# Transposing the last stage's first token group with TensorE, inside an expert's second product, in place of a DMA transpose

## The chip, the cores and the metric

The kernel runs on one core of a Trainium2 chip. The metric is the device time of one execution in microseconds (us). A core has five engines with a queue of instructions each: TensorE (PE; its weight loads are listed as PEld), VectorE (DVE), ScalarE (ACT), GpSimd (POOL) and SyncE (SP). Each works through its own queue in order and waits for others by semaphores; DMA transfers are issued from SP, ACT and POOL.

## The reference

Three stages, on 4 x 576 = 2304 tokens of 512 features:

```python
# 1. sparse attention: scores within tau of the row's maximum stay, then softmax, then @ v
# 2. sticky mixture of experts (8 experts, 512 -> 1024 -> 512): a token takes its own argmax
#    expert or keeps the one of the token before it
out[b, s] = p[e] * (np.maximum(x[b, s] @ w1[e], 0.0) @ w2[e])
# 3. feed-forward with a normalization ahead of it and a residual
mu = np.mean(x, axis=-1, keepdims=True)
var = np.mean((x - mu) ** 2, axis=-1, keepdims=True)
xn = (x - mu) / np.sqrt(var + 1e-06) * g_ln
ch = np.maximum(xn @ w_ch1, 0.0) @ w_ch2          # 512 -> 2048 -> 512
return x + ch
```

## The kernel before, in words

All products are made from pairs of float16 numbers: a value is split into a high part (ACT, a copy with a scale) and the rest (DVE, value minus high part), and a product takes three matmuls (high by high, high by rest, rest by high).

The order of work on each engine is the order in which the Python code records it; the tile pools add the waits on buffers. The part around the change is the loop over `i` in `range(ND0)`, six *single* units `u = E + i` (units 8 to 13). A unit is 128 tokens, sorted by expert, of one expert:

- `s1_unit(u, k)`, for `k` 0 and 1: four blocks of 128 hidden columns each of the first product (line 1012, PE, into a PSUM bank `a`, of which the pool `pa` has four). ACT writes the high part of `hid` (line 1016), DVE the rest (line 1017).
- `t_unit(u + 1)`: the next unit's gathered rows `xg` are transposed by TensorE from float32 (line 987, four transposes into one bank `a`), and split into `xT` by ACT (line 988) and DVE (line 989).
- `s2_unit(u, 0, ...)`: the second product, 24 matmuls into a bank `y` (line 1033), three for each of eight blocks of hidden columns. The first of the three takes the high part of `hid`, the second the rest. Then ACT scales `y` into `yb` (line 1039), and POOL scatters `yb` into the DRAM buffer `ys_d` (line 1041).
- `drip(n)`: brings up to `n` parts of later units' weights in. A part is a float32 block `stg` that a DMA of SP has loaded (lines 199 and 203; the pool has five such buffers), which ACT and DVE split into `w` (lines 124 and 125); the freed buffer is loaded again at once. Now and then the part is half of a block of the last stage's weights `fw`: three DVE steps on `xn` (lines 142, 144, 146), and at the next call of `drip` its split by ACT (line 179) and DVE (line 180), which the list `late` holds.

The last stage takes the tokens in `NG` = 9 groups of 256. For a group `g`, `f_load` reads it from `ys_d` into `xf`, `f_norm` makes mean and reciprocal deviation (DVE and ACT, lines 1080 to 1092), `f_split` normalizes each 128 tokens into `xn` (DVE, line 1101) and splits them into the float16 pair `f16` (ACT line 1102, DVE line 1103), and `f_x` transposes that pair by one DMA issued from ACT's queue into `nT` (line 1109). `halve(2 * g)` makes the first product from `nT` (`f_1`, line 1123: eight banks `a`, 24 matmuls each, with ACT line 1126 and DVE line 1127 behind each), and records the load, normalization and transpose of group `g + 1` on the way. `halve(2 * g + 1)` makes the second product (`f_2`, line 1136), adds the residual (line 1140) and scatters to the output (line 1141).

Units and halves alternate: unit 8, unit 9, half 0, unit 10, half 1, unit 11, half 2, and so on. The first group has no half ahead of it in which to be prepared: its load stands ahead of unit 8, and its normalization, split and transpose inside unit 9 (`i == 1`). From there half 0 begins as soon as unit 9's second product is issued and `nT` is written.

Of the kernel before, what the change touches and what calls it, by code (L numbers as in the profile page):

```python
# [8 lines left out]
F32 = mybir.dt.float32  # L9
F16 = mybir.dt.float16  # L10
I32 = mybir.dt.int32
BF16 = mybir.dt.bfloat16
AF = mybir.ActivationFunctionType
ALU = mybir.AluOpType
# [6 lines left out]
def kernel(  # L21
# [15 lines left out]
    nc = tc.nc  # L37
    B, H, S, D = q.shape
    E, DM, F = w1.shape
# [24 lines left out]
    ident = const.tile([128, 128], F32, name="ident")  # L64
# [119 lines left out]
    P, wt = {}, {}  # L184

    def weights(u, n):

        if (u, n) not in wt:
            sh = [128, 2, DM // 128, F] if n == 0 else [128, 2, F // 128, DM]
            nm = f"w{n}{u % 2}"  # L190
            wt[u, n] = P["wb_p" if u % 2 else "wa_p"][n].tile(sh, F16, name=nm, tag=nm)
        return wt[u, n]
# [37 lines left out]
    if True:  # L230
# [536 lines left out]
        for w, slot in enumerate((0, 1, 2, 3, 4, 5, 7, 8, 9, 11, 12)):  # L767
            for a in range(2):
                g = []
# [23 lines left out]
    V = nc.vector  # L793
# [96 lines left out]
    def tiles(u):  # L890

        if u in PAIRS:
            return PAIRS[u]
        return (2 * u, 2 * u + 1) if u < E else (E + u,)
# [4 lines left out]
    def gather(u):  # L899
        us[u, "g"] = []  # L900
        for n, c in enumerate(tiles(u)):
            xg = P["xgs"][u % 2 if single(u) else n]
            ix, R = (etb, NT - S) if u == "a" else (P["tb"], NT)
            nc.gpsimd.indirect_dma_start(
                out=xg[:], out_offset=None, in_=x_d[0:R, :], in_offset=bass.IndirectOffsetOnAxis(ap=ix[:, c:c + 1], axis=0),
                bounds_check=R - 1, oob_is_err=False)
            us[u, "g"].append(xg)
# [12 lines left out]
    for u in range(E + ND0):  # L920
        fq += [(u, j) for j in range(8)]
        n = 0 if u == 0 else 1
# [6 lines left out]
    def more(n=1):  # L929
        for _ in range(min(n, len(fq))):  # L930
            k = fq.pop(0)
            if k[0] == "f":
                parts[k] = ffn_half(*k[1:])
            else:
                fetch(*k)

    late = []

    def drip(n=1):

        if late:
            next(late.pop(), None)
        for _ in range(n):
            for k in pq:
                if k[0] == 1 and "wb_p" not in P:
                    return
                if k in parts and (not late if k[0] == "f" else k[0] < 2 or (k[0] - 2, k[1] // 4) in done):
                    break
                if k[0] != "f":
                    return  # L950
            else:
                return
            pq.remove(k)
            if k[0] == "f":
                late.append(parts.pop(k))
                next(late[0])
            else:
                parts.pop(k)()
            more()
# [13 lines left out]
    def ready(u, n):  # L973
        while (u, 4 * n + 3) in pq:
            drip()
# [4 lines left out]
    def t_unit(u):  # L980

        new_x(u)
        x = us[u, "x"]
        for n, xg in enumerate(us.pop((u, "g"))):
            t = P["pa"].tile([128, 4, 128], F32, name="a")
            for c in range(4):
                nc.tensor.transpose(t[:, c, :], xg[:, 128 * c:128 * c + 128], ident)
            nc.scalar.activation(out=x[:, 0, n], in_=t, func=AF.Copy, scale=64.0)
            V.scalar_tensor_tensor(out=x[:, 1, n], in0=t, scalar=64.0, in1=x[:, 0, n], op0=ALU.mult, op1=ALU.subtract)
# [29 lines left out]
    def s2_steps(u, i, between=lambda: None):  # L1019
        hid = us[u, "h"]  # L1020
        two = u in PAIRS
        wu = i if two else u
        t2 = weights(wu, 1)
        c = tiles(u)[i]
        if i == 0 or two:
            ready(wu, 1)
        if (two or i + 1 == len(tiles(u))) and u != "a":
            done.add((wu, 1))
        ps = P["py"].tile([128, DM], F32, name="y")
        n = 0  # L1030
        for f in range(8):
            for x, a in ((0, 0), (1, 0), (0, 1)):
                nc.tensor.matmul(ps, hid[:, x, f, 128 * i:128 * i + 128], t2[:, a, f, :], start=(n == 0), stop=(n == 23))  # L1033
                n += 1
            yield
        between()
        tb, tp, dx = (etb, etp, edx) if u == "a" else (P["tb"], P["tp"], P["didx"])
        yb = P["u_p"].tile([128, DM + 1], F32, name="yb", bufs=2)
        nc.scalar.activation(out=yb[:, 0:DM], in_=ps, func=AF.Copy, scale=tp[:, c:c + 1])
        nc.gpsimd.tensor_copy(out=yb.bitcast(I32)[:, DM:DM + 1], in_=tb[:, c:c + 1])  # L1040
        nc.gpsimd.indirect_dma_start(
            out=ys_d[:], out_offset=bass.IndirectOffsetOnAxis(ap=dx[:, c:c + 1], axis=0),
            in_=yb[:], in_offset=None, bounds_check=NT - 1, oob_is_err=False)

    def s1_unit(u, k):
        for _ in s1_steps(u, k):
            pass

    def s2_unit(u, i, between):
        for _ in s2_steps(u, i, between):  # L1050
            pass
# [16 lines left out]
    fs = {}  # L1068
# [6 lines left out]
    def f_norm(g):  # L1075
# [16 lines left out]
        V.reciprocal(out=rs, in_=rs)  # L1092
        fs[g, "n"] = (mv, rs)

    def f_split(g):
        xf = fs[g]
        mv, rs = fs.pop((g, "n"))
        n16 = P["n_p"].tile([128, 2, 2, DM], F16, name="f16")
        for t in range(2):
            xn = P["n_p"].tile([128, DM], F32, name="xn", tag="xn")  # L1100
            V.tensor_scalar(out=xn, in0=xf[:, t, 0:DM], scalar1=mv[:, t, 0:1], scalar2=rs[:, t:t + 1], op0=ALU.subtract, op1=ALU.mult)
            nc.scalar.activation(out=n16[:, 0, t], in_=xn, func=AF.Copy, scale=4.0)
            V.scalar_tensor_tensor(out=n16[:, 1, t], in0=xn, scalar=4.0, in1=n16[:, 0, t], op0=ALU.mult, op1=ALU.subtract)
        fs[g, "s"] = n16

    def f_x(g):
        n16 = fs.pop((g, "s"))
        nT = P["f_p"].tile([128, 2, 2, 4, 128], F16, name="nT")
        nc.scalar.dma_start_transpose(out=nT.rearrange("p a t c n -> p (a t c) n"), in_=n16.rearrange("p a t d -> p (a t d)"))
        fs[g, "x"] = nT  # L1110
# [36 lines left out]
    def halve(h, known=0):  # L1147

        g, b = divmod(h, 2)
        if b == 0:  # L1150
            for fb in range(8):
                f_1(g, fb)
                if fb < 5: drip()
                if g < NG - 1:
                    if fb == 1 and g >= known: f_load(g + 1)
                    if fb == 5 and g >= known: f_norm(g + 1)
                    if fb == 6: f_split(g + 1)
            if g < NG - 1:
                f_x(g + 1)
        else:  # L1160
            f_2(g, 0, drip)
            f_2(g, 1, drip)

    with tc.manual_schedule():
# [35 lines left out]
        g = -1  # L1200
# [72 lines left out]
        while bgp:  # L1273
            n = len(bgp)
# [34 lines left out]
        for i in range(ND0):  # L1309
            u = E + i  # L1310
            for k in range(2):
                s1_unit(u, k)
                if i == 1:
                    if late:
                        next(late.pop(), None)
                    (f_norm, f_split)[k](0)
                drip(1)
            if i + 1 < ND0:
                t_unit(u + 1)
                if i == 1:  # L1320
                    f_x(0)
                if i + 3 < ND0:
                    gather(u + 3)
            s2_unit(u, 0, lambda: drip(2))
            if i:
                halve(i - 1)
        for h in range(ND0 - 1, 2 * NG):
# [3 lines left out]
        def rest(i):  # L1331

            u = E + i
            with tc.If(nd > i):
                with tc.manual_schedule():
                    gather(u)
                    for j in range(5):
                        fetch(u, j)
                    t_unit(u)
                    for j in range(8):  # L1340
                        parts.pop((u, j))()
                        if j < 3:
                            fetch(u, j + 5)
                    for k in range(2):
                        s1_unit(u, k)
                    s2_unit(u, 0, lambda: None)
                    if i + 1 < NDYN:
                        rest(i + 1)
                    if i == ND0:
                        f_load(0)  # L1350
                        f_load(1)
                        f_norm(1)
                        f_norm(0)
                        f_split(0)
                        f_x(0)
                        for h in range(2 * NG):
                            halve(h, 1)
# [31 lines left out]
```

## Time and profile before

| | us |
|---|---|
| median of 3 runs | 1061.17 |
| lowest, highest | 1057.99, 1061.48 |
| the profiled execution | 1058.6 |
| its span, first to last instruction | 1056.8 |
| TensorE busy | 991.1 |
| VectorE busy | 653.4 |
| ScalarE busy | 505.6 |
| TensorE's wait for `nT` of group 0 | 6.2 |

The 1.8 us by which the profiled execution is longer than its span lie around the program's instructions. TensorE is busy for 94% of the span; where it stands still, all others have room, so what counts is what it waits for. Times in the rows are from the start of the span.

### The profile page before, as it was taken

To read this page: it belongs to the slowest core of one execution; us is meant where nothing else is said; L and a number is where in the kernel's file an instruction comes from. 1 tells how busy PE (TensorE), PEld (TensorE's weight loads), DVE (VectorE), ACT (ScalarE), POOL (GpSimd) and SP (SyncE) were. 2 spreads that over 40 slices of the span, in tenths; PEclk is the share of its full clock that TensorE was granted. 3 is DMA by queue.
4 is the path that set the end of the run, shared out by engine and by line. 5 is a ranking of instruction groups with operands and counts; after the bars stand their busy time and mean duration, and the time that the engine had idled before them with its cause. 6 is when DMAs were issued, how large, how long until landed. Compare 5 with 4: busy or idle time off the path is not lost. (4 is left out here: it accounts for less than half of the span.)

```text
span 1056.8 us, 23743 instructions
## 1 busy us (share of the span) xinstructions
PE 991.1 (94%) x9938; PEld 729.0 (69%) x9938; DVE 653.4 (62%) x1127; ACT 505.6 (48%) x791; POOL 391.1 (37%) x411
## 2 busy tenths in 40 slices
PE   6899998998999888899999979999999999999995
PEld 3678877787888776766677657584758668577572
DVE  7788888988897778797787667273334133131220
ACT  4688786786777665465576545243212011111010
POOL 3699897797788671352222300101000000000000
PEclk8999999999999999999999989999999999999998
DMA  7556544464442747578889755364111210111100
GB/s 178 140 136 158 131 103 126 116 156 133 106 93 47 193 134 225 189 241 283 267 298 292 263 181 158 120 205 117 37 31 31 61 31 31 44 37 41 30 12 23
DMA packets 124533, 137.34 MB, mean 130 GB/s; under 512 B 67450, under 2 KB 88954, under 8 KB 124416
## 3 DMA queue, kind: packets, MB, share of 16 engines
q1 hardware_dynamic: 98336, 116.43, 38.2%
q0 software_dynamic: 4960, 14.17, 3.7%
q10 hardware_dynamic: 21120, 5.13, 2.3%
q8 instruction: 79, 1.29, 0.5%
q14 instruction: 38, 0.31, 0.1%
HBM read 100.17 MB, written 19.94 MB: 114 GB/s over the span
## 5 line engine op out<-in xcount | busy, mean ns | idle before, releaser
L1123 PE MATMUL a<-nT,fw 128*128 128x256 f16 x1728 | 191.5, 274 | 6.2 <-DMA nT<-f 6.2
L459 POOL TENSOR_TENSOR hl<-em,hl 128x576 f16<-128x576 f32 x128 | 169.5, 1325 | 54.0 <-ACT hl L458 52.8
L1123 PEld LDWEIGHTS <-fw 128*128 128x128 f16 x1728 | 169.7, 98 | 28.6 <-issue 6.7
L1136 PE MATMUL y<-fw,hid 128*128 128x512 f16 x864 | 187.9, 379 | 0.0
L1136 PEld LDWEIGHTS <-hid 128*128 128x128 f16 x864 | 84.6, 98 | 100.4
L125 DVE SCALAR_TENSOR_TENSOR w<-stg,w 128x1024 f16<-128x1024 f32 x112 | 135.3, 1231 | 17.3 <-ACT w L124 16.6
L1126 ACT ACTIVATE hid<-a 128x512 f16<-128x512 f32 x72 | 42.7, 593 | 214.9 <-PE a L1123 213.0
L446 ACT ACTIVATE e<-s,t 128x576 f32<-128x576 f32 x144 | 106.1, 737 | 70.3 <-PE s L441 57.6
L1141 POOL DMA_INDIRECT out_dram<-xf x18 | 19.1, 1059 | 311.7 <-DVE xf L1140 311.7
L1012 PE MATMUL a<-xT,w 128*128 128x128 f16 (+1 forms) x1536 | 121.5, 241 | 1.5 <-DVE w L125 0.9
L1033 PE MATMUL y<-w,hid 128*128 128x512 f16 x528 | 117.7, 379 | 3.8 <-DVE hid L1017 3.3
L1012 PEld LDWEIGHTS <-w 128*128 128x128 f16 x1536 | 112.3, 99 | 11.3 <-DVE w L125 1.0
L403 DVE TENSOR_REDUCE mc<-sm 128x1 f32<-128x576 f32 x138 | 103.6, 751 | 24.8 <-PE sm L399 22.8
L124 ACT ACTIVATE w<-stg 128x1024 f16<-128x1024 f32 x112 | 114.5, 1051 | 7.7 <-DMA stg<-in_moe_w_dram 3.8
L452 DVE SCALAR_TENSOR_TENSOR em<-s,e 128x576 f32<-128x576 f32 x144 | 107.1, 745 | 9.7 <-POOL hl L459 8.5
L1127 DVE SCALAR_TENSOR_TENSOR hid<-a,hid 128x512 f16<-128x512 f32 x72 | 49.6, 688 | 101.5 <-ACT hid L1126 101.5
L1140 DVE SCALAR_TENSOR_TENSOR xf<-y,xf 128x512 f32<-128x512 f32 x18 | 12.5, 692 | 146.7 <-PE y L1136 146.7
L399 PE MATMUL sm<-qkt 128*128 128x288 f16 (+1 forms) x308 | 75.4, 291 | 24.3 <-DVE mc L403 21.4
L458 ACT ACTIVATE hl<-em 128x576 f16<-128x576 f32 x128 | 86.9, 679 | 18.9 <-DVE em L452 18.5
L1033 PEld LDWEIGHTS <-hid 128*128 128x128 f16 x528 | 50.9, 98 | 63.3 <-DVE hid L1017 5.1
L436 PE MATMUL s<-qkt 128*128 128x288 f16 (+1 forms) x320 | 90.2, 290 | 3.8 <-DVE em L452 3.1
L441 PE MATMUL s<-th,ind 128*128 128x128 bf16 (+5 forms) x960 | 92.0, 206 | 0.0
(290 smaller groups left out, 1797.6 us busy)
## 6 DMA issues: line engine op xcount, KB each, us to landing
stg<-in_moe_w_dram SPq DMA_DIRECT2D x112, 512.0 KB
stg<-in_moe_w_ch_dram SPq DMA_DIRECT2D x32, 512.0 KB
ys_d<-stg SPq DMA_DIRECT2D x6, 769.5 KB
xf<-ys_d SPq DMA_DIRECT2D x9, 513.0 KB
x_d<-xc SPq DMA_DIRECT2D x16, 256.0 KB
ku<-qkt SPq DMA_DIRECT2D x28, 144.0 KB
rawq<-in_q_dram SPq DMA_DIRECT2D x7, 512.0 KB
rawk<-in_k_dram SPq DMA_DIRECT2D x7, 512.0 KB
```

Of the source, the lines that this page charges most:

```text
L124: nc.scalar.activation(out=dst[:, 0, n], in_=t, func=AF.Copy, scale=scale)
L125: nc.vector.scalar_tensor_tensor(out=dst[:, 1, n], in0=t, scalar=scale, in1=dst[:, 0, n], op0=ALU.mult, op1=ALU.subtract)
L403: nc.vector.tensor_reduce(out=mcs[p % 2][:, j:j + 1], in_=mms.pop((p, j))[:, W0:W0 + 576], op=ALU.max, axis=AX.X)
L436: mm(o[:, W0 + 288 * c:W0 + 288 * c + 288], (kt, ku)[k][:, n], y, start=(k == 0), stop=False)
L441: mm(o[:, W0 + i:W0 + i + w], ind[:, t % 4, 0:o.shape[0]], y, start=False, stop=(i == of[-1][0]))
L446: nc.scalar.activation(out=e, in_=mst[p, j][:, W0:W0 + 576], func=AF.Exp, bias=t0, scale=SC)
L452: nc.vector.scalar_tensor_tensor(out=em, in0=ps[:, W0:W0 + 576], scalar=0.0, in1=e, op0=ALU.is_ge, op1=ALU.mult)
L459: nc.gpsimd.tensor_tensor(out=hl[:, 1], in0=em, in1=hl[:, 0], op=ALU.subtract)
L1012: nc.tensor.matmul(ps[:, f, :], t1[:, a, c, fc], x[:, h, i:i + N // 128, c, :], start=(n == 0), stop=(n == 11))
L1033: nc.tensor.matmul(ps, hid[:, x, f, 128 * i:128 * i + 128], t2[:, a, f, :], start=(n == 0), stop=(n == 23))
L1123: nc.tensor.matmul(ps[:, f, :], fw1[:, a, c, fc], x[:, h, :, c, :], start=(n == 0), stop=(n == 11))
L1136: nc.tensor.matmul(ps, hid[:, x, f, ts_], fw2[:, a, f, :], start=(n == 0), stop=(n == 47))
```

## The change

In unit 9 (`i == 1`), `f_split(0)` gives way to `f_rows(0)`: the two normalizations on DVE write float32 rows into one tile, and nothing is split there. `f_x(0)` goes. In its place `f_turn(0)` is recorded inside unit 9's second product, behind the fifth of its eight blocks: eight transposes by TensorE from the float32 rows, four into each of two banks `a`, and for each bank a split into `nT` by ACT and DVE, with the factor 4 that `f_split` applied. The call that finished a `late` half ahead of `f_norm` and `f_split` goes too; `drip` finishes it. Groups 1 to 8 are as before.

```diff
+    def f_rows(g):
+        xf = fs[g]
+        mv, rs = fs.pop((g, "n"))
+        xr = P["n_p"].tile([128, 2, DM], F32, name="f16", tag="f16")
+        for t in range(2):
+            V.tensor_scalar(out=xr[:, t], in0=xf[:, t, 0:DM], scalar1=mv[:, t, 0:1], scalar2=rs[:, t:t + 1], op0=ALU.subtract, op1=ALU.mult)
+        fs[g, "r"] = xr
+
+    def f_turn(g):
+        nT = P["f_p"].tile([128, 2, 2, 4, 128], F16, name="nT")
+        xr = fs.pop((g, "r"))
+        for n in range(2):
+            t = P["pa"].tile([128, 4, 128], F32, name="a")
+            for c in range(4):
+                nc.tensor.transpose(t[:, c, :], xr[:, n, 128 * c:128 * c + 128], ident)
+            nc.scalar.activation(out=nT[:, 0, n], in_=t, func=AF.Copy, scale=4.0)
+            V.scalar_tensor_tensor(out=nT[:, 1, n], in0=t, scalar=4.0, in1=nT[:, 0, n], op0=ALU.mult, op1=ALU.subtract)
+        fs[g, "x"] = nT
...
             for k in range(2):
                 s1_unit(u, k)
                 if i == 1:
-                    if late:
-                        next(late.pop(), None)
-                    (f_norm, f_split)[k](0)
+                    (f_norm, f_rows)[k](0)
                 drip(1)
             if i + 1 < ND0:
                 t_unit(u + 1)
-                if i == 1:
-                    f_x(0)
                 if i + 3 < ND0:
                     gather(u + 3)
-            s2_unit(u, 0, lambda: drip(2))
+            for n, _ in enumerate(s2_steps(u, 0, lambda: drip(2))):
+                if i == 1 and n == 4:
+                    f_turn(0)
```

How it moves VectorE's instructions in unit 9, between the rest of `hid` for unit 9 and the first rest of `hid` for half 0: the kernel before, with `f_10580` the pair `f16`, and `w_10589` unit 10's first weights.

```order
L1017 SCALAR_TENSOR_TENSOR hid<-a,hid 128x4x128
L180 SCALAR_TENSOR_TENSOR fw_97<-xn,fw_97 128x512
L1101 TENSOR_SCALAR xn<-xf,mv,rs 128x512
L1103 SCALAR_TENSOR_TENSOR f_10580<-xn,f_10580 128x512
L1101 TENSOR_SCALAR xn<-xf,mv,rs 128x512
L1103 SCALAR_TENSOR_TENSOR f_10580<-xn,f_10580 128x512
L125 SCALAR_TENSOR_TENSOR w_10589<-stg,w_10589 128x1024
L989 SCALAR_TENSOR_TENSOR xT<-a,xT 128x512
L125 SCALAR_TENSOR_TENSOR w_10589<-stg,w_10589 128x1024 x2
L1127 SCALAR_TENSOR_TENSOR hid<-a,hid 128x512
```

The same stretch of VectorE in the changed kernel (`f_10578` are the float32 rows, line 1113 is the rest of `nT`, line 1148 the rest of half 0's `hid`):

```order
L1017 SCALAR_TENSOR_TENSOR hid<-a,hid 128x4x128
L1101 TENSOR_SCALAR f_10578<-xf,mv,rs 128x512 x2
L180 SCALAR_TENSOR_TENSOR fw_97<-xn,fw_97 128x512
L125 SCALAR_TENSOR_TENSOR w_10583<-stg,w_10583 128x1024
L989 SCALAR_TENSOR_TENSOR xT<-a,xT 128x512
L1113 SCALAR_TENSOR_TENSOR nT<-a,nT 128x512 x2
L125 SCALAR_TENSOR_TENSOR w_10583<-stg,w_10583 128x1024 x2
L1148 SCALAR_TENSOR_TENSOR hid<-a,hid 128x512
```

The two normalizations stand one behind the other and ahead of `fw`; the two subtractions have moved from ahead of a weight split and `xT` to behind them.

ScalarE over the same stretch, the kernel before:

```order
L1016 ACTIVATE hid<-a 128x4x128
L179 ACTIVATE fw_97<-xn 128x512
L1102 ACTIVATE f_10580<-xn 128x512 x2
L124 ACTIVATE w_10589<-stg 128x1024
L988 ACTIVATE xT<-a 128x512
L1109 DMA_TRANSPOSE nT<-f_10580 128x16x128
L124 ACTIVATE w_10589<-stg 128x1024 x2
L1039 ACTIVATE yb<-y,tp 128x512
```

And ScalarE in the changed kernel (line 1112 is the high part of `nT`):

```order
L1016 ACTIVATE hid<-a 128x4x128
L179 ACTIVATE fw_97<-xn 128x512
L124 ACTIVATE w_10583<-stg 128x1024
L988 ACTIVATE xT<-a 128x512
L1112 ACTIVATE nT<-a 128x512 x2
L124 ACTIVATE w_10583<-stg 128x1024 x2
L1039 ACTIVATE yb<-y,tp 128x512
```

The issue of the transposing DMA is gone from ScalarE's queue, and the two copies now stand behind the weight split and `xT`.

TensorE in the changed kernel, from the fifth block's last matmul in unit 9's second product:

```order
L1033 LDWEIGHTS hid
L1033 MATMUL y<-w_10334,hid 128x512
L1111 MATMUL a<-ident,f_10578 128x128 x8
L1033 LDWEIGHTS hid
L1033 MATMUL y<-w_10334,hid 128x512
```

The eight transposes stand between the fifth and the sixth block; nine matmuls of the product follow them, and then half 0, which before followed the same product with nothing in between.

## Rows read from the trace of the kernel before

**Rows 1.** TensorE's waits from 560 to 700 us: line, releaser, total, times, longest

```profile
PE a L1123 <- DMA nT<-f: 6.2, 1, 6.2
```

**Rows 2.** Timeline of TensorE: start, length, what; wait before it and releaser

```profile
613.36 2.55 PE L1033 MATMUL y<-w,hid 128*128 128x512 f16 x11 [1.12 <-DVE hid L1017]
622.09 22.56 PE L1123 MATMUL a<-nT,fw 128*128 128x256 f16 x192 [6.19 <-DMA nT<-f]
...
688.37 21.12 PE L1123 MATMUL a<-nT,fw 128*128 128x256 f16 x192
```

**Rows 3.** Timeline of VectorE, ScalarE and ACT's DMA queue, unit 9

```profile
612.61 0.68 DVE L1017 SCALAR_TENSOR_TENSOR hid<-a,hid 128x512 f16<-128x512 f32 x1
612.73 0.63 ACT L179 ACTIVATE fw<-xn 128x512 f16<-128x512 f32 x1 [2.46 <-DVE xn L146]
...
617.21 1.04 ACT L124 ACTIVATE w<-stg 128x1024 f16<-128x1024 f32 x1
618.05 1.70 ACTq L1109 DMA_TRANSPOSE nT<-f  x1
618.15 0.58 ACT L988 ACTIVATE xT<-a 128x512 f16<-128x512 f32 x1
618.28 1.22 DVE L125 SCALAR_TENSOR_TENSOR w<-stg,w 128x1024 f16<-128x1024 f32 x1 [0.26 <-ACT w L124]
619.42 0.68 DVE L989 SCALAR_TENSOR_TENSOR xT<-a,xT 128x512 f16<-128x512 f32 x1
```

**Rows 4.** Stretches around the pause: engines' busy us (count), granted clock, DMA share, GB/s

```profile
613.00:613.50 0.50, 0.14 (x1) 0.11 (x2) 0.41 (x2) 0.36 (x1) 0.00 (x0) 1.00 0.00 0
618.00:618.50 0.50, 0.00 (x0) 0.00 (x0) 0.24 (x2) 0.50 (x2) 0.00 (x0) 0.74 0.00 0
624.50:625.00 0.50, 0.50 (x4) 0.35 (x3) 0.00 (x0) 0.00 (x0) 0.00 (x0) 0.50 1.06 397
625.50:626.00 0.50, 0.50 (x7) 0.46 (x5) 0.00 (x0) 0.00 (x0) 0.00 (x0) 1.00 0.86 311
```

**Rows 5.** Timeline elsewhere, of VectorE, TensorE and ScalarE: steps like the added ones

```profile
644.11 0.54 DVE L1101 TENSOR_SCALAR xn<-xf,mv,rs 128x512 f32<-128x512 f32 x1
...
685.63 0.68 DVE L989 SCALAR_TENSOR_TENSOR xT<-a,xT 128x512 f16<-128x512 f32 x1
686.24 1.22 DVE L125 SCALAR_TENSOR_TENSOR w<-stg,w 128x1024 f16<-128x1024 f32 x1
...
559.97 1.04 PE L987 MATMUL a<-ident,xg 128*128 128x128 f32 x8
560.85 10.52 PE L1033 MATMUL y<-w,hid 128*128 128x512 f16 x48
...
588.23 0.62 ACT L179 ACTIVATE fw<-xn 128x512 f16<-128x512 f32 x1
588.75 2.94 ACT L124 ACTIVATE w<-stg 128x1024 f16<-128x1024 f32 x3
```

**Rows 6.** Other pauses of TensorE, in its timeline

```profile
8.44 1.35 PE L344 MATMUL s<-ident,qkt 128*128 128x128 f16 x18 [2.83 <-DVE qkt L335]
11.74 0.45 PE L399 MATMUL sm<-qkt 128*64 128x288 f16 x1 [1.95 <-ACT qkt L350]
434.03 2.55 PE L1033 MATMUL y<-w,hid 128*128 128x512 f16 x11 [1.53 <-DVE hid L1017]
```

**Rows 7.** Stretches with those pauses, columns as in rows 4

```profile
10.00:11.00 1.00, 0.00 (x0) 0.00 (x0) 1.00 (x1) 1.00 (x2) 0.99 (x2) 0.83 0.99 337
434.00:436.00 2.00, 1.97 (x10) 0.91 (x11) 0.69 (x1) 0.03 (x1) 0.00 (x0) 1.00 0.90 332
```

**Rows 8.** The rest of the program after half 0, columns as in rows 4

```profile
644.00:1045.00 401.00, 398.96 (x2898) 267.22 (x2896) 129.98 (x225) 80.58 (x128) 24.26 (x26) 1.00 0.20 60
```

**Rows 9.** Timeline of SP: load issues, and ScalarE's split that meets the last of them

```profile
612.73 10.93 SPq L203 DMA_DIRECT2D stg<-in_moe_w_dram  x4
...
637.32 1.05 ACT L124 ACTIVATE w<-stg 128x1024 f16<-128x1024 f32 x1
```

## The prediction

> **What bounds the kernel now.** I read the share of busy time first: TensorE is busy for 94% of the span, so the question is where it stands still. The waits of TensorE from 560 to 700 us then show one that stands out, 6.2 us, once, for the DMA that writes `nT` [rows 1]. Its timeline gives the place: unit 9's second product runs on to 613.36 + 2.55 = 615.91, and half 0 begins at 622.09 [rows 2]. The reader should see two costs there. One is the pause. The other is in the length of half 0's first product: its 192 matmuls take 22.56 us after the pause, and the same 192 take 21.12 us in half 2 [rows 2]. The difference, 1.44 us, is the clock: it is granted in full until about 618.2, some 2.3 us after the last matmul, and stands at 0.50 (1.2 of 2.4 GHz) until about 625 [rows 4]. Together 6.2 + 1.4 = 7.6 us is all that this place can give.
>
> What happens in the pause is a chain over two engines and a DMA. VectorE and ScalarE take turns for the two halves of the group (normalize, copy, subtract), and only behind a weight split and `xT` on ScalarE is the DMA issued; issue and flight take from 618.05 to 622.09, 4.0 us [rows 3]. After half 0 TensorE hardly waits: from 644 to 1045 us it is busy for 398.96 of 401.00 us, at the full clock [rows 8]. What half 0 gains at its start is therefore gained at the end, unless something that does not move with TensorE stands in the way.
>
> **The change part by part.**
>
> *Removed.* On ScalarE two copies of 128x512, on VectorE two subtractions, and one DMA transpose. The DMA is worth 4.0 us of the chain.
>
> *Added.* On VectorE and ScalarE the same number of steps in the same shape, now read from PSUM, as `xT`'s are: 0.58 and 0.68 us each [rows 3]. On TensorE eight float32 transposes. Eight of that form stand in the trace, and what follows them starts 560.85 - 559.97 = 0.88 us after them [rows 5]. TensorE was waiting in any case, so these 0.88 us shorten a pause and cost nothing on the path unless the pause falls under 0.88.
>
> *The new chain.* All that stands ahead of it on VectorE is unchanged, so the rest of unit 9's `hid` starts at 612.61 as before [rows 3]. A step behind one that it does not depend on starts 0.61 later for this length (686.24 - 685.63) [rows 5]. Normalization one: 613.22 to 613.76, with 0.54 each [rows 5]; two: to 614.30. Then the moved `fw` subtraction, which I take at 0.69 from `xT`'s of the same size: to 614.99. The weight split starts there if ScalarE's half of it is ready: `fw` is copied from 612.73 [rows 3], the next split starts 0.52 behind such a copy [rows 5], so at 613.25, and takes 1.04: 614.29, ready. From the weight split's start to `xT`'s is 619.42 - 618.28 = 1.14 [rows 3]: `xT` at 616.13. The first subtraction for `nT` 0.61 behind it: 616.74; the second 0.68 later: 617.42 to 618.10. Half 0 can begin at about 618.15.
>
> *TensorE and ScalarE must not be later than that.* TensorE restarts at 613.36 with 11 matmuls to go [rows 2], two of them in the fifth block, at 10.52 / 48 = 0.22 each [rows 5]: the transposes can start at 613.8, where the first rows have just been written; the second four wait for 614.30 by about 0.1. They end at about 614.9, and the nine matmuls behind them at about 615.91 + 0.88 + 0.1 = 616.9. ScalarE finishes its weight split at 614.29 and `xT` at about 614.8, and makes the two copies by about 616.0, before VectorE asks for them at 616.7. So VectorE is the engine that ends last, and the pause is 618.15 - 616.9 = 1.25 us in place of 6.19.
>
> *The added wait.* Behind the transposes on TensorE's queue stand nine matmuls, and behind these `yb`, its scatter and half 0. Their delay of 1.0 us moves `yb`, which in the trace was not waited for by TensorE, and which is still earlier than before, when it stood behind the DMA's issue.
>
> *The moved weight split.* It needs its load landed by 613.25. In the 0.5 us from 613.0 the DMA engines moved nothing [rows 4], and SP issues in order, the four loads of unit 10's first weights ahead of the row of four at 612.73 [rows 9], so these had landed. The call of `late` that was removed costs nothing: the same `fw` steps stand on both engines, 1.1 us later on VectorE, and its pair is read only in the last stage's second products.
>
> *The clock.* A pause of 1.53 us at 432.5 to 434.0 left the granted clock at 1.00 [rows 6, 7]. A pause of 1.95 us before 11.74 did not: it stood at 0.83 in that us, on its way down [rows 6, 7]. The new pause lies below the first, so I take the clock as kept and the 1.44 us as gained; if it falls they are lost, and nothing in the rows makes it more than that.
>
> *The sum.* 622.09 - 618.15 = 3.9, and 1.4 of clock: 5.4 us. From both sides: VectorE's spacings could be 0.3 us off each way; with the clock lost it is 4.0; with the pause closed by more overlap than I count it is at most 6.6, since `nT` cannot come before TensorE's own 616.9. Against the profiled execution: 1058.6 - 5.4 = 1053.2 us. That execution lies near the lower end of the runs; from the median, 1061.17 - 5.4 = 1055.8. The mean of the three runs and the profiled one is 1059.8, which gives 1054.4. I forecast 1055.0 us, between the three.
>
> **The rivals.**
>
> *The clock falls all the same* (gain 4.0 us; 1059.8 - 4.0 = about 1056). For it speaks the trace's start: TensorE pauses 2.83 us, makes 18 transposes in 1.35 us, pauses again, and the clock falls during that second pause [rows 6, 7], as if the transposes had not counted as work. If transposes are left out here, TensorE has 1.12 us of waiting before 613.36, 0.9 + 0.1 of transposes at 613.8 and 1.25 of pause at the end, with few matmuls between. Against it: the transposes lie between matmuls here, and the pause alone is shorter than the one that the clock survived. The Trainium skill has this as a rule ("TensorE: Matmul & The Clock Gate", section "Part 4: PE-mode transpose"): a transpose does not count as TensorE being busy in the way that a matmul does. By that rule the sum would be 4.0, and the start of the trace agrees with it; the middle of the product shows no such case.
>
> *The pause stays for another reason* (gain about 0.7 us; about 1059). The chain now runs behind a weight split on both engines. If the load behind that split landed only at 617.2, when the trace before made its split, `nT` would be finished 1.14 + 1.07 + 0.61 + 0.68 + 0.68 = 4.2 us later, at 621.4. Against it is the stretch without any transfer [rows 4].
>
> *The gain is given back later* (about 1060 to 1061). Half 0 and all after it come 5 us earlier, while loads take their own time. But ScalarE's and VectorE's steps in half 0 follow TensorE's banks, and the loads are issued as soon as VectorE frees a buffer, so most of it moves along; 2 us in 401 are not busy [rows 8], which leaves little that could absorb.
>
> *Slower than before.* In half 0, ScalarE's split of a weight part stands ahead of its next copy of `hid`. If the part has not landed, the copy waits, the four banks `a` fill, and TensorE stops with its clock falling. The last of unit 10's loads is issued at 612.73 + 10.93 - 0.38 = 623.3, and its split stands at 637.3: 14.0 us [rows 9]. In the changed kernel that load can go out when the third weight split is done, behind `nT`, at about 620.5, and the split comes at 637.3 - 5.4 = 631.9: 11.4 us. Slower begins only where that landing takes 11.4 + 5.4 = 16.8 us and more (some 20 us for 3 us of loss, 1064), and four banks of slack come on top. The median landing is not in my rows, but the four loads together take 10.9 us to issue, each behind a freed buffer, and nothing waits for one in half 0. I hold it for very unlikely.
>
> **How the numbers follow.** Forecast 0.64, clock lost 0.16, pause stays 0.08, given back 0.08, slower 0.04. A measurement of this kernel can tell about 0.3%, or 3.2 us, from no change. The forecast lies 2.2 us above that in gain, and runs differ by up to 3.5 us (1057.99 to 1061.48), so of its 0.64 some 0.58 come out as faster; of the clock's case, 0.8 us above the bound, 0.12; of the two small gains 0.03 by spread. Faster 0.73, same 0.22, slower 0.05. The range goes from the lowest run less the largest gain, 1057.99 - 6.6 = 1051.4, rounded to 1051.5, to where a pause that stays begins to be told from nothing, 1060.4.
>
> **What would show it.** Right: TensorE's wait at half 0's first matmul is 1 to 1.6 us, and its releaser is VectorE's line 1113, not a DMA; the eight transposes take 0.9 to 1.1 us with a wait of 0.1 between; the granted clock stays 1.00 from 612 to 640, and half 0's 192 matmuls take 21.1 us; half 0 begins near 618.2. The clock's case: the same start, but 22.5 us. The weight split's case: VectorE's line 125 of unit 10 starts after 616 with ScalarE's line 124 waiting for a DMA. Given back: new waits of TensorE after 640 that add to over 2 us. The forecast is wrong if the new pause is over 2.5 us, or if the distance from half 0's first matmul to the end of the span, 434.7 us before, is not shorter by the 1.4 us of clock.

## The result, and the profile after

| | before | changed |
|---|---|---|
| median, first comparison (14 runs each) | 1060.88 us | 1051.35 us |
| lowest to highest | 1057.28 to 1063.62 | 1049.26 to 1057.5 |
| ratio, 95% interval | | 0.9915 [0.9901, 0.9929] |
| ratio in two later comparisons | | 0.9947 [0.9926, 0.9968], 0.9922 [0.9906, 0.9938] |
| the profiled execution, its span | 1058.6, 1056.8 | 1051.45, 1049.7 |

Faster, as forecast, but by more: 9.5 us between the medians of the first comparison against a forecast of about 5.4, and 0.15 us below the range's lower end. Over all runs (89 of the kernel before, 27 of the changed one, in five and three sets) the means are 1060.20 and 1052.59, 7.6 us apart with a standard error of 0.4. In the first comparison the means are 8.2 us apart, so of the 9.5 us 1.3 come from taking medians and 0.6 from the draw of those runs; 2.2 us are missing in the forecast.

The waits of TensorE in the changed kernel over the whole span (line, releaser, total, times, longest), to be held against [rows 1]:

```profile
PE y L1033 <- DVE hid L1017: 2.7, 3, 1.5
...
PE a L1144 <- DVE nT L1113: 0.8, 1, 0.8
```

The wait for the DMA is gone from the list, and in its place stands a wait for VectorE's second subtraction, 0.8 us long. (The first line counts waits of the whole span; one of 0.86 us lies at this place, as one of 1.12 did before.) TensorE's timeline of the changed kernel through that place, to be held against [rows 2]:

```profile
609.08 2.97 PE L1033 MATMUL y<-w,hid 128*128 128x512 f16 x13
612.91 0.60 PE L1033 MATMUL y<-w,hid 128*128 128x512 f16 x2 [0.86 <-DVE hid L1017]
613.45 1.08 PE L1111 MATMUL a<-ident,f 128*128 128x128 f32 x8
614.37 2.11 PE L1033 MATMUL y<-w,hid 128*128 128x512 f16 x9
616.31 0.27 PE L1144 MATMUL a<-nT,fw 128*128 128x256 f16 x1
617.35 21.01 PE L1144 MATMUL a<-nT,fw 128*128 128x256 f16 x191 [0.76 <-DVE nT L1113]
638.20 5.52 PE L1012 MATMUL a<-xT,w 128*128 128x128 f16 x96
```

The reader sees the eight transposes cost 614.37 - 613.45 = 0.92 us, half 0's first matmul go out as soon as the product is done (it needs the high part of `nT` only), and the other 191 follow after 0.76 us at their full pace, 21.01 us. VectorE and ScalarE in the changed kernel, against [rows 3]:

```profile
612.16 0.68 DVE L1017 SCALAR_TENSOR_TENSOR hid<-a,hid 128x512 f16<-128x512 f32 x1
...
612.77 0.99 DVE L1101 TENSOR_SCALAR f<-xf,mv,rs 128x512 f32<-128x512 f32 x2
...
613.67 0.69 DVE L180 SCALAR_TENSOR_TENSOR fw<-xn,fw 128x512 f16<-128x512 f32 x1
...
614.24 1.07 ACT L1112 ACTIVATE nT<-a 128x512 f16<-128x512 f32 x2
614.28 1.22 DVE L125 SCALAR_TENSOR_TENSOR w<-stg,w 128x1024 f16<-128x1024 f32 x1
...
615.41 0.68 DVE L989 SCALAR_TENSOR_TENSOR xT<-a,xT 128x512 f16<-128x512 f32 x1
616.01 1.28 DVE L1113 SCALAR_TENSOR_TENSOR nT<-a,nT 128x512 f16<-128x512 f32 x2
```

The order is the one worked out: ScalarE has its two copies at 615.3, and VectorE's weight split and `xT` hold the subtractions back until 616.01. The granted clock over the pause in the changed kernel, with the columns of [rows 4] (behind the five engines: clock, DMA share, GB/s):

```profile
616.00:617.00 1.00, 0.59 (x4) 0.20 (x2) 1.00 (x3) 1.00 (x2) 0.00 (x0) 1.00 0.63 33
617.00:618.00 1.00, 0.65 (x7) 0.58 (x6) 1.00 (x2) 0.79 (x2) 0.00 (x0) 1.00 0.75 229
618.00:619.00 1.00, 1.00 (x12) 0.90 (x10) 1.00 (x2) 0.00 (x0) 0.46 (x1) 1.00 0.64 248
```

It stays at 1.00, the 2.4 GHz level, through the whole place.

### The profile page after: what moved, and what is told of

It is laid out like the page before. It is cut to its first block, busy times and chain, and to the rows that moved or that the text cites. A ratio compares the mean times of both kernels' runs of the same rounds, so it can differ in the third digit from the quotient of the medians.

```text
span 1049.7 us, 23757 instructions
## 1 busy us (share of the span) xinstructions
PE 990.2 (94%) x9946; PEld 728.9 (69%) x9946; DVE 652.8 (62%) x1127; ACT 505.1 (48%) x791; POOL 392.8 (37%) x411
## 5 line engine op out<-in xcount | busy, mean ns | idle before, releaser
L1161 DVE SCALAR_TENSOR_TENSOR xf<-y,xf 128x512 f32<-128x512 f32 x18 | 12.5, 692 | 146.8 <-PE y L1157 146.8
```

## The experiments

Several of the expectations speak of theory 1: the clock lost after the pause costs more in most executions than in the first profile.

**The kernel before, once more** (no edit).

> The kernel before once more, unchanged, so that each of its runs comes with its mean granted clock. Theory 1 (the clock's share of the pause varies): the price of the clock after the pause was 1.4 us in the profiled execution and is 3 to 5 us in the runs of 1061 us and more; then the runs split into a group near 1058 and one near 1061, the slower ones have a mean granted clock lower by about 0.0014 per 3 us, and the profiled pause itself stays 6.2 us. Theory 2 (the spread is unrelated to the clock): time and mean granted clock do not go together over the runs.

Measured: 0.9998 [0.9983, 1.0013]; its profiled run took 1061.56 us. TensorE in it, at half 0:

```profile
623.65 23.66 PE L1123 MATMUL a<-nT,fw 128*128 128x256 f16 x192 [6.12 <-DMA nT<-f]
647.15 5.52 PE L1012 MATMUL a<-xT,w 128*128 128x128 f16 x96
```

Its granted clock (columns as above):

```profile
618.00:619.00 1.00, 0.00 (x0) 0.00 (x0) 0.30 (x2) 0.70 (x2) 0.00 (x0) 1.00 0.00 0
622.00:622.50 0.50, 0.00 (x0) 0.00 (x0) 0.00 (x0) 0.50 (x2) 0.00 (x0) 0.57 1.27 289
...
628.50:629.00 0.50, 0.50 (x5) 0.37 (x3) 0.00 (x0) 0.03 (x1) 0.00 (x0) 0.61 0.88 344
```

The pause is the same, 6.1 us, but the clock fell only at 622.1, 1.6 us before TensorE resumed, and came back at 628.9. The product took 23.66 us, so 2.54 us of clock in place of 1.44. That is more than in the first profile, but short of the 3 to 5 us expected for a run of 1061 us and more. Time and mean granted clock go together: of 28 runs of the kernel before in this comparison the five fastest average 1057.75 us at 0.985, the five slowest 1063.31 at 0.979. The two groups of runs that I expected are not there, though, and most of the spread comes from elsewhere: this profile is 2.9 us longer than the first, 1.9 of which lie ahead of unit 9's second product (611.16 against 609.27).

**The kernel before, two more profiles** (no edit).

> The kernel before, one more profile of it. Theory (in the pause ahead of half 0 the clock stays low for a fixed stretch of 6.8 us, seen in the first two profiles, but begins at a different moment of the pause in each execution): the low stretch is 6.8 us again, its start lies anywhere from 2 us behind the last matmul to the pause's end, and half 0's first product takes 21.12 us plus half of what of the stretch falls on it, between 21.6 and 24.5 us. Rival (the price of the first profile is the usual one): 22.5 us.

> The kernel before, a fourth profile of it, with the same expectations as the third: a low stretch of 6.8 us and 21.6 to 24.5 us by where it begins; 22.5 us by the rival.

Measured, in one row of TensorE's timeline each:

```profile
624.15 23.56 PE L1123 MATMUL a<-nT,fw 128*128 128x256 f16 x192 [6.31 <-DMA nT<-f]
```

```profile
622.63 23.54 PE L1123 MATMUL a<-nT,fw 128*128 128x256 f16 x192 [6.13 <-DMA nT<-f]
```

The granted clock at the fall, in the first and then the second of these:

```profile
622.25:622.50 0.25, 0.00 (x0) 0.00 (x0) 0.00 (x0) 0.25 (x1) 0.00 (x0) 0.72 1.28 292
```

```profile
620.75:621.00 0.25, 0.00 (x0) 0.00 (x0) 0.00 (x0) 0.25 (x1) 0.00 (x0) 0.58 1.28 292
```

A step of 0.25 us with a mean between 0.50 and 1.00 tells where in it the clock changed. So read, fall and return are at 618.24 and 625.07 in the first profile of the kernel before, 622.07 and 628.90, 622.36 and 629.19, 620.79 and 627.62 in the other three: 6.83 us each. Half of what lies behind half 0's first matmul is 1.49, 2.63, 2.52 and 2.50 us; the products took 1.44, 2.54, 2.44 and 2.42 us over 21.12. So in these four profiles the low stretch had one length while its place in the pause changed, and the profile from which I took the price was the cheapest of the four. The mean is 2.2 us.

**Matmuls in the pause: the wait stays, its clock is kept.**

```diff
             s2_unit(u, 0, lambda: drip(2))
+            if i == 1:
+                ft = P["pa"].tile([128, 4, 128], F32, name="a")
+                for _ in range(26):
+                    nc.tensor.matmul(ft, ones16, ones16.unsqueeze(1).to_broadcast([128, 4, 128]))
             if i:
                 halve(i - 1)
```

> The kernel before, with 26 extra matmuls of ones (0.22 us each, 5.6 us) on TensorE in the pause ahead of half 0, into a bank that nobody reads. The wait for the DMA transpose stays, only its clock is kept. Theory 1: the granted clock stays 1.00 from 616 to 640, half 0's first product takes 21.1 us, the profiled run is 1.4 us under the kernel before and the median 2 to 4 us under it, and the slow group of runs thins out. Theory 2 (the median's extra gain comes from elsewhere): 1.4 us in profile and median alike. If the clock were of no weight: no change.

Measured: 0.9965 [0.9953, 0.9977], 3.7 us. TensorE's timeline:

```profile
618.73 5.78 PE L1328 MATMUL a<-ones 128*128 128x512 f16 x26
625.06 21.12 PE L1123 MATMUL a<-nT,fw 128*128 128x256 f16 x192 [0.55 <-DMA nT<-f]
```

The granted clock over half 0's product:

```profile
625.00:646.00 21.00, 20.94 (x192) 18.80 (x193) 14.79 (x25) 9.37 (x14) 1.02 (x1) 1.00 0.67 230
```

Half 0 begins where it did, 12.5 us behind the start of unit 9's second product, and its product runs in 21.12 us. The filled pause is thus worth 2.4 to 5.0 us in the runs. Not all of that is the clock of half 0's product: unit 10 is 0.85 us shorter here as well (11.30 us from its first matmul to half 1, against 12.15; below). The profiled run, expected 1.4 us under the kernel before, took 1059.2 us, since its unit 9 reached the second product only at 612.52; from there to the end of the span it is 3.4 us shorter than the kernel before.

**Transposes in the pause**: the same edit with `for c in range(52): nc.tensor.transpose(ft[:, c % 4, :], ident, ident)`.

> The kernel before, with 52 extra float32 transposes of the identity (0.11 us each, 5.7 us) on TensorE in the pause ahead of half 0, in place of the 26 matmuls tried earlier. By the rule that a transpose does not count as TensorE being busy: the granted clock falls to 0.50 during them and half 0's first product takes 22.5 to 23.7 us, the time as the kernel before. Rival, that transposes count as matmuls do: the clock stays 1.00, the product takes 21.1 us, and the median is 3 to 4 us under the kernel before as with the 26 matmuls.

Measured: 0.9977 [0.9958, 0.9996]. TensorE's timeline, and the clock at the end of the transposes:

```profile
620.85 5.84 PE L1328 MATMUL a<-ident 128*128 128x128 f32 x52
627.22 21.12 PE L1123 MATMUL a<-nT,fw 128*128 128x256 f16 x192 [0.53 <-DMA nT<-f]
```

```profile
624.00:626.60 2.60, 2.60 (x25) 2.45 (x23) 1.82 (x3) 1.70 (x2) 0.00 (x0) 1.00 1.00 227
```

After 5.8 us of nothing but transposes the clock is still granted in full. The rule of the Trainium skill ("TensorE: Matmul & The Clock Gate", section "Part 4: PE-mode transpose") that a transpose does not count as TensorE being busy is not borne out for these float32 transposes; the measurement decides. (The trace lists them as MATMUL and does not show in which mode they ran.) The rival that I built on it has no ground here. I had taken it from the 18 float16 transposes at the start of the trace [rows 6]; no run tried that type, and why the clock fell there stays open. The median is 2.7 us under the kernel before, short of the 3 to 4 expected, with an interval that holds both.

**The transposes at the end of the product**: `n == 7` in place of `n == 4`.

> The changed kernel, with the transposes recorded behind the last block of unit 9's second product instead of the fifth. Theory A (the place in the middle counts): TensorE transposes from about 615.1 to 616.0, ScalarE copies to 617.1, VectorE's subtractions end near 618.2, so the pause ahead of half 0 is about 2 us in place of 0.8 and the time 0.9 to 1.2 us above the changed kernel's; with the clock fallen 1.4 us more. Theory B (VectorE's weight split and xT set the end wherever the transposes stand): no change within 0.3 us in the profile.

Measured: 1053.26 us, 0.9942 [0.9923, 0.9961]. TensorE's timeline:

```profile
609.55 2.97 PE L1033 MATMUL y<-w,hid 128*128 128x512 f16 x13
...
616.03 1.04 PE L1111 MATMUL a<-ident,f 128*128 128x128 f32 x8
617.80 0.27 PE L1144 MATMUL a<-nT,fw 128*128 128x256 f16 x1 [0.74 <-ACT nT L1112]
618.64 21.01 PE L1144 MATMUL a<-nT,fw 128*128 128x256 f16 x191 [0.57 <-DVE nT L1113]
```

From the start of the product to the 191 matmuls it is 9.09 us, against 8.27, 8.53 and 8.53 in the three profiles of the changed kernel. The two of 8.53 have the same wait of 1.12 us ahead of the product's last part as this one, so the fair difference is 0.56 us: the place in the middle counts, as theory A says, for about half of the expected 0.9 to 1.2. The clock stays.

**The order without TensorE's transposes**: `f_split` and the DMA kept, unit 9's two weight calls behind the fifth block of its second product, `f_x(0)` ahead of `t_unit(u + 1)`.

> The kernel before with its DMA transpose kept, but the order of the better version: unit 9's two weight calls moved behind the fifth block of its second product, and the DMA issued ahead of the next unit's transposes. Theory A (both the order and TensorE's transposes count): the pair is split by about 614.5, the DMA takes 4 us, half 0 begins at about 618.7, some 9.5 us behind the start of unit 9's second product (12.8 before, 8.3 changed), the pause is 4 to 4.5 us and the clock still falls; 3 to 4 us under the kernel before. Rival (the order alone carries the gain, the DMA is cheap): half 0 begins within 0.5 us of the changed kernel's and the time equals the changed kernel's.

Measured: 1057.68 us, 0.9971 [0.9955, 0.9988], 3.1 us. TensorE's timeline:

```profile
610.11 5.34 PE L1033 MATMUL y<-w,hid 128*128 128x512 f16 x24
619.66 24.04 PE L1123 MATMUL a<-nT,fw 128*128 128x256 f16 x192 [4.21 <-DMA nT<-f]
```

Half 0 begins 9.55 us behind the product's start, as theory A had it, and a pause of 4.2 us still loses the clock, here at its dearest: 24.04 - 21.12 = 2.9 us, since the fall came 0.8 us before the resumption:

```profile
618.75:619.00 0.25, 0.00 (x0) 0.00 (x0) 0.25 (x2) 0.00 (x0) 0.00 (x0) 0.68 1.00 214
```

Order alone gives some two fifths of the gain. The same order with TensorE's transposes in place of the DMA is the next run: there the pause is gone, and with it the loss of clock.

**The changed kernel with unit 9's weight calls moved behind the transposes** (three times, beside the changed kernel in two).

```diff
                 if i == 1:
                     (f_norm, f_rows)[k](0)
-                drip(1)
+                else:
+                    drip(1)
...
                 if i == 1 and n == 4:
                     f_turn(0)
+                    drip(1)
+                    drip(1)
```

> The changed kernel, with unit 9's two calls that split a weight part moved from between its first-product halves to directly behind the transposes. Nothing but xT then stands ahead of nT on VectorE, and the three steps on the last stage's weights no longer stand ahead of the rest of unit 9's hid. Theory A: both pauses left around unit 9's second product go (0.86 at 612.9 and 0.76 at 617.4), 1.5 us less than the changed kernel, about 1050 us. Rival: the weight splits now stand in a row of three ahead of half 0's first hid copy on ScalarE and hold TensorE's banks; then TensorE waits in half 0 for a bank and the time is equal or up to 2 us above the changed kernel's.

> The changed kernel once more, on the same chip as the next three and with a second profile. Theory 1 (the pause's price in clock varies between executions of the kernel before, and is gone here): median 8 to 9 us under the kernel before; in the profile the granted clock is 1.00 from 612 to 640 again, half 0's first product takes 21.0 to 21.2 us, and the runs that are slower lost their clock ahead of 420 us. Rival: the clock falls in some executions here too; then its second profile may show 22.5 us or more there.

> The changed kernel with unit 9's two weight calls moved behind the transposes, once more, beside the changed kernel on one chip. From the first profile (half 0 begins 6.06 us behind the start of unit 9's second product, against 8.27): 2.2 us under the changed kernel. Rival: the first medians (ratios 0.9918 and 0.9915 against the kernel before) were the truth and the 2.2 us are given back later: no difference.

> The changed kernel a third time, beside the version with the weight calls moved. If the trace's account holds (4.5 us of pause, 1.4 to 2.9 of clock, 0.8 of later waits): 6.7 to 8.2 us under the kernel before in the median, between the two earlier ratios of 0.9915 and 0.9947.

> The changed kernel with unit 9's two weight calls moved behind the transposes, a third time. By its profiles 2.0 to 2.3 us under the changed kernel of the same call; by the rival (given back later) equal to it.

TensorE's timeline of the first of these:

```profile
608.21 3.40 PE L1033 MATMUL y<-w,hid 128*128 128x512 f16 x15
611.45 1.04 PE L1111 MATMUL a<-ident,f 128*128 128x128 f32 x8
612.32 2.11 PE L1033 MATMUL y<-w,hid 128*128 128x512 f16 x9
614.27 21.12 PE L1144 MATMUL a<-nT,fw 128*128 128x256 f16 x192
```

TensorE waits for nothing here; half 0 begins 6.06 us behind the product's start in all three profiles, against 8.27, 8.53 and 8.53 in the changed kernel's. The medians: 1050.5 (0.9918 [0.9899, 0.9937]); then 1050.93 beside 1053.56 for the changed kernel; then 1051.22 (0.9910 [0.9888, 0.9931]) beside 1052.29; so 2.6 and 1.1 us less, where I expected 2.2 and 2.0 to 2.3. Over all runs, 18 and 27, it is 1051.26 against 1052.59: 1.3 us with a standard error of 0.6. The traces show 2.2 to 2.5 us gained at the place, and from half 1 to the end of the span both take as long (399.7 to 400.1 us); the runs point the same way but do not settle the size. The changed kernel itself kept its clock in all three profiles, 21.0 us for the 191 matmuls each time. Its second set came out 6.7 us under the kernel before in the medians, where I expected 8 to 9, and its third 8.8, where I expected 6.7 to 8.2.

**All profiles held together.** Unit 9's second product starts anywhere from 608.21 to 614.64 us in the fourteen profiles, in no order that follows the kernels. Counting from that start to the end of the span leaves this spread out, and then profiles of one kernel agree within 1.0 us:

| | profiles | from there to the end of the span, us | mean under the kernel before |
|---|---|---|---|
| kernel before | 4 | 447.5, 448.5, 448.5, 448.5 | |
| the order without TensorE's transposes | 1 | 445.8 | 2.5 |
| transposes in the pause | 1 | 445.2 | 3.1 |
| matmuls in the pause | 1 | 444.9 | 3.4 |
| transposes at the end of the product | 1 | 441.9 | 6.4 |
| changed kernel | 3 | 440.6, 441.2, 441.3 | 7.3 |
| weight calls behind the transposes | 3 | 438.6, 438.5, 439.0 | 9.6 |

The first of the four is 1.0 us shorter than the others: that is its cheaper clock.

## Why the prediction came out as it did

*Bound and mechanism*: right. The place, the chain, the new releaser (VectorE's line 1113), the transposes between the blocks, the clock kept, the gain carried to the end: each of these is in the profile after as named. Of the signs that I set, three were off in size: TensorE waits 0.76 us for the second subtraction, not 1 to 1.6; half 0's 191 matmuls begin at 617.35, not near 618.2; and there is no wait between the transposes. The terms of the sum were too small. By the trace, four profiles of the kernel before and three of the changed one, on the average:

| term | forecast | measured |
|---|---|---|
| half 0 begins earlier, against the start of unit 9's second product | 3.9 | 12.69 - 8.33 = 4.36 |
| clock in half 0's first product | 1.4 | 2.21 |
| unit 10, from its first matmul to half 1 | 0 | 12.15 - 11.78 = 0.37 |
| from there to the end of the span | 0 | 400.27 - 399.97 = 0.30 |
| sum | 5.4 | 7.24 |

(8.33 counts the one matmul that goes out early as 0.11 us of the product.) The sum lies within the standard error of the 7.6 us of all runs. The last term is hardly more than the spread: it was 399.7 to 400.1 us in the changed kernel's profiles and 400.2 to 400.4 in the others', but also 400.1 and 400.4 in the two with a filled pause. That it belongs to the change is not shown.

*The clock*, the step that failed: "nothing in the rows makes it more than that", and with it that 7.6 us is all that the place can give and 6.6 us the most that the change can. The rows of one execution did not bound it. In the four profiles the low stretch is as long each time, but where in the pause it starts differs, and the price runs from the 1.44 us of that profile to 2.54, and 2.9 with the pause of 4.2 us. Nor is 7.6 us all: with the weight calls moved as well, the traces show 9.6: half 0 begins 12.69 - 6.06 = 6.6 us earlier there, since the wait ahead of the last part of unit 9's product goes too. I had even the hint: the profiled execution stood near the fast end of its runs, and I took that for spread of no concern to the sum.

*The pause*: my VectorE chain took several steps at their full length where the next one began before they ended: the two normalizations (0.99 us for both, where I had 0.54 each), the `fw` step (0.61 to the next start, where I had 0.69) and the two subtractions (1.28, where I had 0.68 each). From the rest of `hid` to the end of `nT` it is 617.29 - 612.16 = 5.1 us, where I had 5.5. The early first matmul gives another 0.1.

*Later waits*, which I had at nothing: in unit 10, TensorE waits 0.3 to 0.6 us for ScalarE's high part of `hid` in each profile of the kernel before, and 0.2 or less in the changed one. In the first profile of each:

```profile
650.94 0.39 PE L1033 MATMUL y<-w,hid 128*128 128x512 f16 x1 [0.49 <-ACT hid L1016]
```

```profile
644.27 0.39 PE L1033 MATMUL y<-w,hid 128*128 128x512 f16 x1
```

It comes from ScalarE's queue, where the issue of group 1's transposing DMA stands ahead of that copy; in the profiles with this wait the copy starts some 0.05 us after the issue ends. The row of the issue in the first profile of the kernel before, then in the changed kernel, then with the matmuls in the pause:

```profile
648.04 2.20 ACTq L1109 DMA_TRANSPOSE nT<-f  x1
```

```profile
641.75 1.82 ACTq L1130 DMA_TRANSPOSE nT<-f  x1
```

```profile
649.57 1.33 ACTq L1109 DMA_TRANSPOSE nT<-f  x1
```

The same instruction, issued in 2.0 to 2.3 us in the kernel before, 1.7 to 1.9 in the changed one, 1.3 in both kernels with a filled pause. Why is open; no run was made on it. A lost clock is not the only thing that makes TensorE wait there: one profile of the moved calls kept its clock and has an issue of 1.70, and still waits 0.50 us, since there the issue itself begins later, 4.07 us behind unit 10's first matmul in place of 3.55.

*The rivals*: the clock did not fall, and float32 transposes hold it. The weight split's load was there (line 125 at 614.28). Nothing was given back, and nothing became slower.

*The forecast of one number*: 1055.0 stood between the profiled execution and the median. The pooled 7.6 us from the median of 1061.17 would have been 1053.6, inside the range; the 14 runs of the first comparison came out another 2 us lower.

## What to carry to other kernels

Price a TensorE pause long enough to lose the clock as its own length plus a clock term that changes from run to run (1.4 to 2.9 us here), and take more than one profile of the kernel before. Where such a pause can be made short enough (0.8 us kept the clock here, 4.2 us lost it), the clock's part comes on top of the part that one counts. Compare profiles from the changed place to the end, so that the spread ahead of it does not hide the effect. When group preparation stands behind bulk work on an in-order engine, move the bulk work behind it first: it costs no instruction, and here it gave about 3 us with the DMA kept and some 1 to 2 more with the transposes.

## What the runs showed of the hardware that was not expected

- In the four profiles of the kernel before and in the one with the earlier DMA (618.84 to 625.67) the granted clock fell to 0.50 in the pause and stood there for 6.83 us, whether 3.0 or 6.0 us of that lay on resumed matmuls.
- 52 float32 transposes in a row, 5.84 us, kept the granted clock at 1.00 as 26 matmuls did.
- The issue of one and the same transposing DMA on ScalarE (group 1's) took from 1.33 us, with a filled pause ahead of half 0, to 2.38 us, with the earlier DMA, and the copy of `hid` behind it on that queue kept TensorE waiting for up to 0.66 us.
